# One fused attention and two-layer kernel: the sums of the first layer's weights, the order of the second block's output products, and when rows are loaded and summed

## The chip, the core and the metric

The kernel runs as one program on one core of a Trainium2 chip. The metric is device time in microseconds of one execution, from the inputs in the chip's main memory to the output there. The engines are named as in the profile: PE does matrix products and transposes (PEld is its load of the stationary operand, which overlaps), DVE, ACT and POOL do elementwise work, SP issues the transfers (DMA). Every engine works through its own instructions in the order in which the program lists them.

## What is computed

Eight batches of eight heads of 576 positions with 64 dimensions. Keys and values are pooled by eight, attention is taken over the 72 pooled positions, and the heads are laid side by side as 4608 rows of 512. Two feed-forward layers follow.

```python
k_p = k.reshape(B, H, Sp, 8, D).mean(axis=3);  v_p likewise
attn = softmax(scale * q @ k_p^T);  x = heads side by side of attn @ v_p      # 4608 x 512
gate = 1 / (1 + exp(-(x @ w_gate)));  val = x @ w_val                         # d_ff 1536
y = (gate * val) @ w_out
h = y @ w_in;  out = where(h > 0, h, exp(min(h, 0)) - 1) @ w_out2             # d_ff 2048
```

The six weight matrices arrive as 64-bit floats, which the kernel narrows itself on DVE (`convert`, and `prepared` for the second layer). A value that goes into a product is kept as two tiles, an upper part and the remainder (`split`: a copy on ACT, then a subtraction on POOL or DVE), and a product of two such values is three matmuls (`PASSES`).

## The kernel before

**Stages.** The rows are worked on in nine blocks of 512. Block 0's attention comes first, while weights arrive (to about 59 us). Then a loop over the twelve chunks `c` of the first layer's hidden columns handles block 0: gate product, value product, and, one chunk late, the output product (`emit_y`). In its first six rounds it also prepares block 1's attention. `plan()` lists what is placed before, between and behind the products of each round. From `LAG_FROM = 6` on, each round also runs two chunks of block 1's gate and value products ("side", L686 into `gw`): `side_gate` puts the sigmoid into a tile `sg1`, `side_val` multiplies and appends a store of the result to `g_dram`. `convert(1)` stands three times in a round and carries the narrowing of the weights three jobs further; it also counts down and issues the delayed stores in `stores`.

After the twelve rounds block 1 has only its output products left, the lagging products. A loop of twelve units does them (L711, into `acc`, weights reloaded as `wos`): `reload` brings one chunk of `g` from `g_dram`, `again` splits it, `emit_y` makes twelve matmuls. The attention of block 2 lies between them through lists `at2`: transposing queries (`emit_q`), scores (`emit_s`), `emit_exp`, `emit_norm`, transposing the probabilities (`emit_t`, with `keep_p` splitting them on ACT and DVE). All of these use one PSUM tile of two banks (`two_banks`, one buffer). The last two chunks of output products are kept as filler.

**Sums of weights.** Blocks 2 to 8 use a two-by-two scheme with seven products in place of eight. It needs sums and differences of weight blocks, which `form_weights` makes for each of twelve units `u`, in six steps each: two sums (L262), four differences half as wide (L264, L265, L269, L270), three splits, and stores to `t_dram`. It is a generator: `work(n)` runs its next n steps, and after it those of `prepared()`, which narrows and combines the second layer's weights. `formed[0]` says up to which pair of chunks the weights may be taken. Before, that is set after all twelve rounds, `work(4)` stands in each unit of the lagging loop, and what is left runs in block 2.

**Blocks 2 to 8.** After the attention products (`weighted`, L648 and L655) `form_x` forms the sums of the rows, through a chain of ACT and DVE operations that reads the products' PSUM banks. Then come twelve units `u` of seven steps `k`, each step being six matmuls into one of three banks (L1323) and a few output products as filler. The sum `u2` behind step 1 (L1338) must be done before step 3 opens the same bank. `thin_plan(m)` hangs the attention of the next block behind steps (u, k), through one PSUM bank (`one_bank`): `q_thin`, `s_thin`, `t_thin`, and for keys and values `load_kv`, `pool_k`/`pool_v` (a DVE reduction each), `place_v`, `k_first`, `k_last`. `WORK_AT` names the steps behind which `work()` stands, 35 in a block, and block 2 has 26 more. `load_t` fetches the stored sums two units ahead into two buffers of the tag "tt". Loaded rows of queries, keys and values, and the copies of the output products, share a tag "row" with three buffers; a load whose buffer is not free holds up SP and all that SP has behind it.

After block 8 the second layer runs (from about 1240 us), which the change does not touch.

## Time and profile before

| | |
|---|---|
| median of 3 runs (lowest to highest) | 2000.53 us (1994.74 to 2003.0) |
| profiled execution, own time | 1999.19 us |
| span of its instructions | 1996.3 us |
| busy: PE, DVE, ACT, POOL | 1821.4, 1096.5, 858.8, 634.0 us |
| mean granted PE clock (share of full speed) | 0.965 |
| attention of block 0 | 0 to 59.7 us |
| rounds 0 to 5, then 6 to 11 | 59.7 to 173.4, then to 291.3 us |
| lagging products, attention products of block 2 | 291.3 to 384 us |
| block 2, from the forming of its rows | 384 to 518.7 us |
| blocks 3 to 7, block 8 | 518.7 to 1120.1 us, to about 1240 us |
| second layer | to 1996.3 us |

The profile is of one execution. A busy PE need not be a PE at its peak: where the granted clock is below 1 each matmul takes longer. So a stretch is judged by three numbers of the windows view together: its length, the time that PE is busy in it, and the clock.

### The profile page before, as it was taken

To read this page: it belongs to the slowest core of one execution; us is meant where nothing else is said; L and a number is where in the kernel's file an instruction comes from. 1 tells how busy PE (TensorE), PEld (TensorE's weight loads), DVE (VectorE), ACT (ScalarE), POOL (GpSimd) and SP (SyncE) were. 2 spreads that over 40 slices of the span, in tenths; PEclk is the share of its full clock that TensorE was granted. 3 is DMA by queue.
4 is the path that set the end of the run, shared out by engine and by line. 5 is a ranking of instruction groups with operands and counts; after the bars stand their busy time and mean duration, and the time that the engine had idled before them with its cause. 6 is when DMAs were issued, how large, how long until landed. Compare 5 with 4: busy or idle time off the path is not lost. (4 is left out here: it accounts for less than half of the span.)

```text
span 1996.3 us, 28241 instructions
## 1 busy us (share of the span) xinstructions
PE 1821.4 (91%) x10308; PEld 1607.7 (81%) x10308; DVE 1096.5 (55%) x2055; ACT 858.8 (43%) x1776; POOL 634.0 (32%) x626
## 2 busy tenths in 40 slices
PE   5668986688899988989999989999999999999999
PEld 4556875577788877878888888999999999999998
DVE  6666625766767666767665655434544344443432
ACT  3343313334454443534445424445454444544543
POOL 2333315443434332433333422222222222222222
PEclk8878997799999999989999999999999999999999
DMA  7334426477676756656666696534334343343431
GB/s 200 102 115 146 153 88 217 150 225 233 231 230 222 226 191 220 220 193 224 204 229 201 211 347 217 209 111 175 111 137 182 114 174 111 133 165 135 161 111 50
DMA packets 154361, 353.10 MB, mean 177 GB/s; under 512 B 48112, under 2 KB 79856, under 8 KB 154224
## 3 DMA queue, kind: packets, MB, share of 16 engines
q1 hardware_dynamic: 154224, 351.32, 51.7%
q8 instruction: 81, 1.33, 0.3%
q14 instruction: 56, 0.46, 0.1%
HBM read 290.46 MB, written 60.82 MB: 176 GB/s over the span
## 5 line engine op out<-in xcount | busy, mean ns | idle before, releaser
L1444 PE MATMUL bank<-form,wr 128*128 128x384 f32 x2016 | 411.0, 338 | 1.1 <-DVE u L1477 0.7
L1444 PEld LDWEIGHTS bank<-form,wr 128*128 128x128 f32 x2016 | 366.5, 188 | 29.1 <-DVE u L1477 1.1
L711 PE MATMUL acc<-g,wos 128*128 128x512 f32 x1152 | 374.1, 410 | 15.1 <-ACT g L95 12.4
L1490 PE MATMUL oacc<-w2o,gc 128*128 128x512 f32 x1080 | 288.9, 393 | 0.4 <-POOL gc L96 0.4
L1490 PEld LDWEIGHTS oacc<-w2o,gc 128*128 128x128 f32 x1080 | 199.6, 187 | 30.4 <-POOL gc L96 0.8
L711 PEld LDWEIGHTS acc<-g,wos 128*128 128x128 f32 x1152 | 197.7, 197 | 29.6 <-ACT g L95 14.0
L1323 PE MATMUL pl<-s,wg 128*128 128x256 f32 x1008 | 159.8, 294 | 39.9 <-DVE u L1338 38.3
L96 POOL TENSOR_TENSOR gc<-ea,gc 128x384 fp32r<-128x384 f32 x96 | 98.0, 1021 | 299.0 <-ACT gc L95 295.9
L1323 PEld LDWEIGHTS pl<-s,wg 128*128 128x128 f32 x1008 | 138.5, 192 | 63.0 <-DVE u L1338 50.9
L96 POOL TENSOR_TENSOR g<-sg,g 128x512 fp32r<-128x512 f32 x108 | 145.9, 1362 | 134.7 <-ACT g L95 130.8
L96 POOL TENSOR_TENSOR gc<-pair,gc 128x384 fp32r<-128x384 f32 x96 | 97.8, 1019 | 260.3 <-ACT gc L95 239.8
L1323 PEld LDWEIGHTS pl<-a,wg 128*128 128x128 f32 x1008 | 142.8, 193 | 18.4 <-ACT r L1034 4.1
L1323 PE MATMUL pl<-a,wg 128*128 128x256 f32 x1008 | 153.4, 289 | 3.6 <-DVE xe L1028 2.1
L1323 PE MATMUL pl<-s,tt 128*128 128x256 f32 x1008 | 151.3, 286 | 1.7 <-DVE sg L1353 1.7
L1323 PEld LDWEIGHTS pl<-s,tt 128*128 128x128 f32 x1008 | 138.6, 189 | 11.3 <-DVE sg L1353 2.1
L1490 PE MATMUL oacc<-w2p,gc 128*128 128x512 f32 x540 | 143.1, 393 | 0.0
L95 ACT ACTIVATE g<-sg 128x512 fp32r<-128x512 f32 x108 | 67.7, 627 | 155.1 <-DVE sg L1363 114.4
L1490 PEld LDWEIGHTS oacc<-w2p,gc 128*128 128x128 f32 x540 | 99.8, 187 | 14.8
L1453 ACT ACTIVATE ea<-bank 128x384 f32<-128x384 f32 x48 | 23.6, 492 | 157.7 <-PE bank L1444 157.7
L1457 DVE SCALAR_TENSOR_TENSOR ea<-ea,bank 128x384 f32<-128x384 f32 x48 | 26.6, 554 | 117.2 <-ACT ea L1454 117.2
L1358 POOL TENSOR_TENSOR sg<-sg,u 128x256 f32<-128x256 f32 x42 | 37.0, 880 | 151.6 <-DVE u L1357 139.8
L686 PE MATMUL gv<-x,wg 128*128 128x512 f32 x288 | 78.6, 428 | 3.6 <-DVE x L96 3.6
(221 smaller groups left out, 3046.8 us busy)
## 6 DMA issues: line engine op xcount, KB each, us to landing
wr<-wd SPq DMA_DIRECT2D x96, 896.0 KB, 5.1
tt<-td SPq DMA_DIRECT2D x84, 768.0 KB, 5.2
wos<-wd SPq DMA_DIRECT2D x96, 512.0 KB, 5.2
rw<-in_moe_w_out_dram SPq DMA_DIRECT2D x22, 512.0 KB, 5.0
r<-yd SPq DMA_DIRECT2D x24, 384.0 KB, 9.0
out_dram<-po SPq DMA_DIRECT2D x36, 256.0 KB, 2.0
rw<-in_moe_w_in_dram SPq DMA_DIRECT2D x16, 512.0 KB, 5.0
wd<-rw SPq DMA_DIRECT2D x16, 512.0 KB, 5.1
```

The costliest lines, as they stand in the source:

```text
L95: nc.scalar.activation(out=dst_hi, in_=src, func=AF.Copy)
L96: eng.tensor_tensor(out=dst_lo, in0=src, in1=f32(dst_hi), op=ALU.subtract)
L686: nc.tensor.matmul(d, lhsT=w[:, i, a_w, j], rhs=x[j][:, a_x], start=(j == 0 and a_w == 0 and a_x == 0), stop=(j == KD - 1 and a_w == 1),)
L711: return lambda: nc.tensor.matmul(acc[m], lhsT=w[:, a_w, m * P:(m + 1) * P], rhs=g[:, a_g], start=(c == 0 and a_w == 0 and a_g == 0), stop ...
L1323: nc.tensor.matmul(src, lhsT=w(a_w, j), rhs=f_t[nm][:, j, a_x], start=opens and m == 0, stop=m == 5, skip_group_check=True,)
L1358: nc.gpsimd.tensor_tensor(out=c22, in0=c22, in1=u4, op=ALU.mult)
L1444: nc.tensor.matmul(bank[b ^ flip], lhsT=wp[q][a_w][:, w, j * P:(j + 1) * P], rhs=form_tile(s, a)[j][:, a_x], start=opens and n == 0, stop= ...
L1453: nc.scalar.activation(out=e, in_=src, func=AF.Relu, scale=-1.0)
L1457: nc.vector.scalar_tensor_tensor(out=e, in0=e, scalar=-1.0, in1=src, op0=ALU.add, op1=ALU.max)
L1490: return lambda: nc.tensor.matmul(acc[t + i], lhsT=g[c][:, a_g, i * P:(i + 1) * P], rhs=wo2[2 * q + e][a_w], start=opens and p == 0, stop= ...
```

## The change

It does five things.

1. `form_weights` starts inside rounds 7 to 11: `formed[0]` rises at the end of each round from 6 on, and rounds have `work(3)`, `work(4)` and, from 6 on, another `work(3)`. The lagging loop has `work(2)` in each of ten units, and a loop finishes the rest before `load_t`. Block 2 keeps only the 35 places. The sums and splits of one unit lie in one tile of the tag "tt" and are split in place; three stores take the place of two.
2. Of block 1's `g`, chunks 10 and 11 are not stored. They stay in the tiles `sg1`, which are now in the tags "p" and "qT" with one buffer each, and the lagging products start with them (`order`), with `wo[10]` and `wo[11]` still on the chip. The others are stored and reloaded two at a time. The delay of a store is two `convert`s in place of one.
3. Block 1's queries are loaded at the beginning into a tile `q1`.
4. The attention of block 2 moves to earlier units: scores at units 0, 2, 4, 6, normalisation at 1, 3, 5, 7, `emit_t` at 3, 5, 7, 9, and the key sums of batch 3 all come within the loop. `emit_k` for that batch takes the place of `k_first` at the start of block 2.
5. In `thin_plan` keys and values are loaded and summed one to a unit, `t_thin` is one step later with DVE's half as a step of its own (`t_low`), `q_thin` is one step later, and `WORK_AT` has other places, again 35.

```diff
-    g_dram = [dram.tile([P, NW], F32, ...) for i in range(C1)]
+    g_dram = [dram.tile([P, 2, NW], F32, ...) for i in range(C1 // 2 - 1)]
...
         for u in range(C1):
             cc, i = divmod(u, 2)
             while formed[0] <= cc:
                 yield
             wa, wb = wg[2 * cc], wg[2 * cc + 1]
-            ra, rb = plain_t().bitcast(F32), plain_t().bitcast(F32)
+            abc = wts.tile([P, 3, NW], F32, name="tw", tag="tt", bufs=2)
+            ra, rb, st = [abc[:, x] for x in range(3)]
...
-            kept()
             yield
             split(flat(wb[:, i, 0, 0:SQ]), flat(wb[:, i, 1, 0:SQ]), ra[:, lo])
...
             yield
-            two = raw_tile("t32")...
-            split(two[:, :, 0], two[:, :, 1], rb.rearrange("p (m f) -> p m f", m=2))
-            store(t_dram[u][:, 0:2], two)
-            yield
-            one = plain_t()...
-            split(one[:, 0], one[:, 1], ra[:, hi])
-            store(t_dram[u][:, 2], one)
+            kept()
+            split(st.bitcast(F32R), rb.bitcast(F32R), rb)
+            yield
+            split(ra[:, lo].bitcast(F32R), ra[:, hi].bitcast(F32R), ra[:, hi])
+
+            def keep_all(u=u, ra=ra, rb=rb, st=st):
+                for s, r in ((0, st), (1, rb)):
+                    nc.sync.dma_start(out=t_dram[u][:, 0:2, s], in_=r...)
+                nc.sync.dma_start(out=t_dram[u][:, 2]..., in_=ra)
+
+            keep.append(keep_all)
             yield
...
-            if i:
-                early[i - 1].append(lambda t=t: load_q(t))
...
+        q1 = spare("q1")
+        for i in range(TPW):
+            load_q(TPW + i, q1[:, i])
...
-            sg = wts.tile([P, NW], F32, name="sg1", tag="tt", bufs=2)
+            sg = at_p.tile([P, NW], F32, name="sg1", tag="qT" if c % 2 else "p")
...
-            stores.append([1, lambda: nc.sync.dma_start(out=g_dram[c], in_=sg)])
+            if c < C1 - 2:
+                stores.append([2, lambda: nc.sync.dma_start(out=g_dram[c // 2][:, c % 2], in_=sg)])
+            else:
+                back[c] = sg
...
             convert(1)
+            work(3)
             if late:
                 one = side_gate(second)
...
             if late:
                 side_val(*one)
             convert(1)
+            work(4)
             if pend is not None:
                 emit_y(0, *pend)
...
             if late:
                 side_val(*side_gate(second + 1))
+                work(3)
+                formed[0] = second // 2 + 1
...
+        again(C1 - 2)
+        while stores:
+            stores.pop(0)[1]()
+        reload(0)
         emit_k(SQ)
         emit_y(0, *pend)
-        while stores:
-            stores.pop(0)[1]()
+        reload(1)
         pt_now[0] = new_pt()
-        formed[0] = C1 // 2
         flush_y(0, acc)
         acc = outputs()
...
+        again(C1 - 1)
         t0 = SQ * TPW
+        emit_q(t0)
+        order = [C1 - 2, C1 - 1] + list(range(C1 - 2))
...
-            q_at, s_at, t_at = ((0, 1, 4), (1, 3, 6), (4, 5, 8), (6, 7, 10))[i]
-            put2(s_at, s2, t)
-            put2(s_at + 1, lambda t=t: emit_norm(t, p2[t]))
-            put2(t_at, emit_t, t)
-        for i in range(TPW):
-            put2((0, 1, 4, 6)[i], emit_q, t0 + i)
-            if i:
-                put2((0, 1, 4, 6)[i] - 1, load_q, t0 + i)
...
-        for c in range(C1):
-            again(c + 1)
-            reload(c + 2)
-            if c < C1 - 2:
-                emit_y(1, acc, g_of[c], c)
-            for f in at2[c]:
-                f()
-            work(4)
+            put2(2 * i, s2, t)
+            put2(2 * i + 1, lambda t=t: emit_norm(t, p2[t]))
+            if i + 1 < TPW:
+                put2(2 * i, load_q, t + 1)
+                put2(2 * i + 1, emit_q, t + 1)
+            put2(2 * i + 3, emit_t, t)
+        for c in range(NCH):
+            put2((1, 2, 3, 4, 5)[c], load_kv, "k", SQ + 1, c)
+            put2((4, 5, 6, 7, 8)[c], pool_k, SQ + 1, c)
+        put2(8, emit_k, SQ + 1)
+        put2(9, load_q, t0 + TPW)
+        for j, c in enumerate(order[:-2]):
+            if j % 2 == 1:
+                reload(j // 2 + 2)
+            for f in at2[j]:
+                f()
+            y = y_steps(acc, g_of[c], c, wo[C1 + c], first=j == 0, last=False)
+            for f in y:
+                f()
+            if j > 1:
+                next_wo()
+            again(order[j + 2])
+            work(2)
+        while stored[0] < C1:
+            work()
...
-                put(u + 2, 0, t_thin, t, 0, HP)
-                put(u + 2, 3, t_thin, t, HP, NCH)
-                put(u, 5, q_thin, t)
+                put(u + 2, 1, t_thin, t, 0, HP)
+                put(u + 2, 2, t_low, t, 0)
+                put(u + 2, 4, t_thin, t, HP, NCH)
+                put(u + 2, 5, t_low, t, HP)
+                put(u, 6, q_thin, t)
...
-                put(*((u - 1, 2) if i else (1, 4)), load_q, t)
-            if m < B:
-                for u, k, c in ((2, 0, 0), (4, 0, 1), (6, 0, 2), (8, 0, 3), (9, 0, 4)):
-                    put(u, k, load_kv, "v", m, c)
...
+                put(u, 0, load_q, t)
+            for c in range(NCH):
+                u = 2 * c + 2
+                if m + 1 < B:
+                    put(u - 1, 1, load_kv, "k", m + 1, c)
+                    put(u, 0, pool_k, m + 1, c)
+                if m < B:
+                    put(u, 2, load_kv, "v", m, c)
+                    put(u + 1, 1, pool_v, m, c)
+                    put(u + 1, 3, place_v, m, c)
             if m + 1 < B:
-                for u, k, c in ((9, 2, 0), (10, 1, 1), (10, 3, 2), (10, 5, 3), (11, 4, 4)):
-                    put(u, k, load_kv, "k", m + 1, c)
-                for u, k, c in ((10, 4, 0), (11, 0, 1), (11, 2, 2), (11, 3, 3)):
-                    put(u, k, pool_k, m + 1, c)
-                put(11, 5, k_first, m + 1)
+                put(10, 6, k_first, m + 1)
+                put(11, 2, k_last, m + 1)
...
-        WORK_AT = {(u, k) for u in range(2, C1, 2) for k in (1, 2, 4, 5)} | {(u, 3) for u in range(1, C1, 2)}
-        WORK_AT -= {(10, 2), (10, 4)}
-        WORK_AT |= {(0, 5), (1, 1), (1, 5), (1, 6), (4, 6), (6, 6), (8, 6), (9, 6), (10, 6), (11, 1), (11, 4)}
+        WORK_AT = {(u, k) for u in range(2, C1, 2) for k in (1, 3, 4, 5, 6)}
+        WORK_AT |= {(u, 3) for u in range(1, C1, 2)} | {(0, 5), (1, 1), (1, 5), (1, 6)}
...
-            else:
-                k_first(n + 1)
...
-                    if (u, k) in WORK_AT or n == SQ and k in (0, 2, 6):
+                    if (u, k) in WORK_AT:
                         work()
```

## Rows read from the trace of the kernel before

**Rows 1.** Windows: length, busy PE PEld DVE ACT POOL, PEclk, DMA share, GB/s
```profile
59.70:173.40 113.70, 75.58 (x359) 62.24 (x357) 81.98 (x116) 50.56 (x83) 43.94 (x34) 0.83 0.39 132
...
193.90:212.90 19.00, 19.00 (x85) 15.73 (x85) 11.74 (x17) 6.16 (x12) 6.43 (x6) 1.00 0.52 174
...
251.00:270.00 19.00, 19.00 (x86) 15.73 (x85) 7.30 (x11) 4.50 (x9) 6.04 (x6) 1.00 0.26 88
...
303.30:367.10 63.80, 46.15 (x188) 36.63 (x189) 38.17 (x56) 21.32 (x45) 33.78 (x30) 0.82 0.56 186
...
393.40:518.70 125.30, 109.44 (x722) 96.98 (x721) 87.10 (x175) 54.79 (x114) 47.99 (x51) 0.96 0.69 224
518.70:637.00 118.30, 110.05 (x770) 98.84 (x769) 82.15 (x171) 56.37 (x125) 45.48 (x49) 1.00 0.69 225
637.00:764.10 127.10, 113.75 (x778) 101.03 (x777) 83.09 (x169) 54.70 (x119) 44.55 (x47) 0.97 0.66 214
...
1004.00:1120.10 116.10, 110.44 (x765) 98.55 (x764) 69.87 (x158) 53.20 (x109) 37.35 (x33) 1.00 0.62 205
```

**Rows 2.** Timeline of PE: start, length, instruction xcount [idle before, its releaser]
```profile
118.63 1.09 PE L564 MATMUL atq<-ident,rq 128*128 128x128 f32 x4 [10.14 <-issue]
...
292.07 3.02 PE L711 MATMUL acc<-g,wo 128*128 128x512 f32 x12
303.29 5.42 PE L711 MATMUL acc<-g,wos 128*128 128x512 f32 x12 [8.20 <-ACT g L95]
...
334.73 0.63 PE L564 MATMUL atq<-ident,rq 128*128 128x128 f32 x4 [2.09 <-issue]
...
349.10 1.09 PE L564 MATMUL atq<-ident,rq 128*128 128x128 f32 x4 [5.12 <-issue]
...
354.08 1.14 PE L572 MATMUL ats<-kbd,qT 128*128 128x144 f32 x8
...
376.71 1.51 PE L648 MATMUL atv<-pt,vbd 128*128 128x128 f32 x6 [8.06 <-DVE pt L96]
...
384.05 2.34 PE L711 MATMUL acc<-g,wos 128*128 128x512 f32 x9
392.63 1.09 PE L1095 MATMUL atk<-ident,ks 128*128 128x128 f32 x4 [6.24 <-DVE xe L1028]
```

**Rows 3.** Timeline of DVE, same columns
```profile
117.77 0.76 DVE L585 TENSOR_TENSOR p<-ats,mx 128x576 f32<-128x576 f32 x1
...
298.22 0.69 DVE L738 COPY yo<-acc 128x512 f32<-128x512 f32 x1 [2.85 <-DMA yd<-yo]
298.83 1.28 DVE L262 TENSOR_TENSOR nt<-wg 128x512 f32<-128x512 f32 x2
...
317.81 2.89 DVE L262 TENSOR_TENSOR nt<-wg 128x512 f32<-128x512 f32 x2 [3.35 <-POOL t L96]
```

**Rows 4.** Groups by line, DVE: count, busy us, mean ns, idle before it by releaser
```profile
L262 DVE TENSOR_TENSOR nt<-wg 128x512 f32<-128x512 f32 x24 | 25.0, 1072 | 17.3 <-POOL t L96 10.7 <-POOL nt L96 6.4
```

**Rows 5.** Transfers by line: count, KB each, median us from issue to landing
```profile
td<-t SPq DMA_DIRECT2D x12, 512.0 KB, 6.5
```

**Rows 6.** Timeline of SP's queue, the start and block 4: time from first issue to last
```profile
24.09 5.94 SPq L419 DMA_DIRECT2D rq<-in_q_dram  x2
38.83 0.34 SPq L133 DMA_DIRECT2D rw<-in_moe_w_out_dram  x1
...
737.55 9.18 SPq L447 DMA_DIRECT2D rkv<-in_k_dram  x2
```

**Rows 7.** Timeline of ACT, the end of block 4
```profile
756.59 0.42 ACT L95 ACTIVATE rs<-nt 128x256 fp32r<-128x256 f32 x1 [5.24 <-DMA wd<-rw]
```

**Rows 8.** Waits of PE, rounds 0 to 5, then blocks: total us, times, longest
```profile
PE atq L564 <- issue: 21.2, 3, 10.1
...
PE pl L1323 <- DVE u L1338: 38.3, 38, 4.2
PE att L626 <- POOL p L619: 12.3, 24, 1.8
```

More of the change, by code (lines that the diff above doesn't have):

```diff
@@ L73, in fused_kernel @@
     y_dram = [dram.tile([P, KD, NB], F32, name=f"yd{i}", tag=f"yd{i}") for i in range(NBLK)]
-    g_dram = [dram.tile([P, NW], F32, name=f"gd{i}", tag=f"gd{i}") for i in range(C1)]
+    g_dram = [dram.tile([P, 2, NW], F32, name=f"gd{i}", tag=f"gd{i}") for i in range(C1 // 2 - 1)]
     t_dram = [dram.tile([P, 3, 2, HW], F32, name=f"td{i}", tag=f"td{i}") for i in range(C1)]
@@ L250, in kept @@
             keep.clear()
-        def store(dst, src):
-            keep.append(lambda: nc.sync.dma_start(out=dst, in_=f32(src)))
         for u in range(C1):
@@ L473, in pool_k @@
         n = size(c)
-        t = at_p.tile([P, 2, D], F32, name="ks", tag="kv", bufs=NCH)
+        t = at_p.tile([P, 2, D], F32, name="ks", tag="kv", bufs=NCH + 1)
         nc.vector.tensor_reduce(out=t[:n, 0], in_=r.rearrange("p (r d) -> p d r", r=POOL), op=ALU.add, axis=AX.X)
@@ L519, in sums_of @@
         if nm == "k":
-            t1 = at_p.tile([P, 2, D], F32, name="ks", tag="kv", bufs=NCH)
+            t1 = at_p.tile([P, 2, D], F32, name="ks", tag="kv", bufs=NCH + 1)
             for e in range(2):
@@ L526, in sums_of @@
             t4 = t4.bitcast(F32R)
-            t1 = at_p.tile([P, 2, D], F32R, name="vhl", tag="kv", bufs=NCH)
+            t1 = at_p.tile([P, 2, D], F32R, name="vhl", tag="kv", bufs=NCH + 1)
             split(t4[:, :, 0, :], t4[:, :, 1, :], four, nc.vector)
@@ L707, in emit_g, with y_steps @@
         return g
-    def y_steps(acc, g, c, w, by_tile=False):
+    def y_steps(acc, g, c, w, by_tile=False, first=None, last=None):
+        first = c == 0 if first is None else first
+        last = c == C1 - 1 if last is None else last
         def one(m, a_w, a_g):
@@ L712, in one @@
                 acc[m], lhsT=w[:, a_w, m * P:(m + 1) * P], rhs=g[:, a_g],
-                start=(c == 0 and a_w == 0 and a_g == 0), stop=(c == C1 - 1 and a_g == 1),
+                start=(first and a_w == 0 and a_g == 0), stop=(last and a_g == 1),
             )
@@ L874, in fused_kernel @@
         lag_ps = []
+        back = {}
         def side(c, i):
@@ L1074, in with_next @@
             return steps[:-1] + [f]
-        for c in (C1 - 2, C1 - 1):
-            fill += with_next(y_steps(acc, g_of[c], c, wo[C1 + c], c == C1 - 1))
+        for c in order[-2:]:
+            fill += with_next(y_steps(acc, g_of[c], c, wo[C1 + c], c == order[-1], False, c == order[-1]))
         filler(9)
@@ L1138, in t_thin, with t_low @@
                 turn_p(t, a, c)
-            keep_p(t, a, c0, c1)
+            o = t % TPW * P
+            hi, lo = [pt_now[0][:, h, c0:c1, o:o + P] for h in range(2)]
+            src = a[:, 0:(c1 - c0) * P].rearrange("p (c n) -> p c n", n=P)
+            nc.scalar.activation(out=hi, in_=src, func=AF.Copy)
+            halves_of[t, c0] = hi, lo, src
+        def t_low(t, c0):
+            hi, lo, src = halves_of.pop((t, c0))
+            nc.vector.tensor_tensor(out=lo, in0=src, in1=f32(hi), op=ALU.subtract)
         def thin_plan(m):
```

62 lines of the change are left out of this document (29 added, 33 removed).

## The prediction

> **What bounds the kernel now.** I read the windows by stage first [rows 1], because a mean over the whole span hides where PE is idle. From block 2 on PE is close to full: block 3 takes 118.30 us, of which PE is busy 110.05 at clock 1.00. So are the side rounds: in round 7 PE is busy all of its 19.00 us. Two stretches are not. In rounds 0 to 5 PE is busy 75.58 of 113.70 us at clock 0.83. The ten lagging units take most of a stretch of 63.80 us in which PE is busy 46.15 us at clock 0.82; DVE (38.17), ACT (21.32) and POOL (33.78) are not full either, so no engine bounds it. (The clock is the granted one as a share of 2.4 GHz; its levels are 1.2 and 2.4, so 0.82 is a mix of both, in stretches where PE pauses.) Next I read PE's timeline for what ended each pause [rows 2]. Where the releaser says only "issue", I looked in DVE's timeline [rows 3] for what ends just before, and the pauses turn out to be queues waiting for each other in program order.
>
> I sum against the profiled execution, 1999.19 us (2.9 us more than its span, 1.3 us less than the median).
>
> **A. Queries at the beginning: +1 us (0 to +3).** The pauses ahead of the query transposes in rounds 0 to 5 look like a late load, but are none. The longest is 10.14 us and ends at 118.63 [rows 2]. DVE ends its subtraction L585, the last reader of the two-bank scores tile, at 117.77 + 0.76 = 118.53 [rows 3]. The transposes write that tile; they wait for DVE, which has narrowing of weights ahead of the subtraction. An earlier load does not alter that, so I count no gain. The cost: two such loads hold SP for 5.94 us at the start [rows 6], and there are now five in place of these two, some 9 us more of SP. SP's next issue is a fetch at 38.83 us [rows 6], so most of it is covered; without that cover it would be the 9 us.
>
> **B. Sums inside rounds 7 to 11: +4 us (0 to +12).** By the steps, 10 of them in each of five rounds, 50 of 74 move here; a round gets 10/6 = 1.67 units. A unit on DVE is two sums and four differences of half the width. Two sums take 1.28 us with POOL idle, 2.89 us with POOL busy [rows 3], and 1.07 us each on average [rows 4]; I take half that for a difference. So a unit is 2.6, 4.3 or 5.8 us and a round gets 4.3, 7.2 or 9.7 us. Round 7 has DVE busy 11.74 of 19.00 us [rows 1], hence 16.0, 18.9 or 21.4 us of 19.0. Rounds 7 to 9 still narrow weights and are alike; round 10 has 7.30 us and stays at 17 us in the worst case. The mean fits exactly, the dear case costs 3 x 2.4 = 7 us, and a full DVE delivers the two multiplications that free PE's banks late now and then. I take 4; the top adds a few microseconds of a lower clock.
>
> Two sums at 1.28 us against 2.89 us [rows 3] are a question of ports. The Trainium skill, SBUF — State Buffer, section Who interferes with whom, says that a DVE instruction with two SBUF inputs and a GpSimd one that reads SBUF exclude each other for a whole instruction; both rows agree. By that rule alone, with a POOL subtraction in the way of every step, this part would be +7, not +4.
>
> Queues passed: SP gets 25 more issues here. A store of sums lands in 6.5 us [rows 5]; the unit that reuses the tile comes seven steps later, over half a round, so its first sum on DVE should find it free. If not, all of DVE's narrowing waits behind that sum. The sigmoids on ACT now wait for the store of the same tile from one round before, half as large and issued by the second `convert` after its multiplication, within about half a round of 19 us. Behind the sigmoid stand ACT's splits, for which the next output products wait. Both at zero, covered by the rest of the round; without that cover up to 6.5 us a round.
>
> **C. The lagging stretch: -17 us (-27 to -6).** Now the first lagging product starts at 303.29 after 8.20 us of idleness, behind a split of a reloaded chunk [rows 2]. Starting from the chip removes the reload, and next is late: the last copy of the finished block leaves PSUM at 298.22 + 0.69 = 298.91 [rows 3], then come a split and the query copy (which waits for it, as both use one tile), some 1.5 us, and scores of 1.14 us [rows 2]. That gives 301.5, 2 us earlier, and one tile's scores are done.
>
> Then ten units. In two of them PE has transposes of about 1.0 (four like them take 0.63 to 1.09), a pause until the two banks are evacuated, 2.09 at best, queries 0.6, scores 1.1 and two times twelve products [rows 2]. At full speed twelve take about 2.9 us (3.02 at 292.07), so the pair takes 10.5 us. Now twelve take 3.0 to 5.4, and the pause grows to 5.12 when DVE and ACT have sums ahead of the evacuation [rows 2]. With 20 steps of sums here, not 48, and L262's waits for POOL's tiles (10.7 + 6.4 us [rows 4]) gone by the new tiles, I take 12 us. Four pairs are 48, unit 0 is 4, unit 9 is 5: the products end at 358.5. The attention products are not held by the last probabilities any more (8.06 us idle [rows 2]), since these are transposed ahead of unit 9's products. They then take what they take now without that pause, 384.05 - 376.71 + 1.5 = 8.9 us, to 367.4 in place of 384.05: -17. At 10.5 us a pair it is -27; at today's pace of 6 us a unit, with only the last pause gone, -6.
>
> **D. The forming of block 2's rows: -4 us (-5 to -1).** `k_first` takes a PSUM bank that the forming chain reads to its end, and PE waits 6.24 us for it [rows 2]. Without it the first two steps of block 2 and their filler use banks freed early in the chain; step three still waits. Bounds: the whole pause or almost nothing.
>
> **E. Block 2 without sums: -8 us (-12 to -3).** It takes 125.30 us against 118.30 of block 3, with 15.9 us idle against 8.3, and clock 0.96 against 1.00, worth 0.04 x 109.44 = 4.4 [rows 1]. Idle and clock make 12. Not all is the sums, so I take 8.
>
> **F. Blocks 3 to 7: -10 us (-21 to +10).** In block 4, 127.10 us, two key loads without a free buffer stretch over 9.18 us in SP's queue [rows 6], the stores behind are late, and ACT waits 5.24 us for one [rows 7]. With one load to a unit a buffer is always free: -6 of the 8.8 us by which block 4 is longer than block 3. PE's waits for normalised probabilities, 12.3 us [rows 8], lose one step of over 1 us each: -9. Query transposes stand one step before the scores that need them, no longer two: +5 (24 times 0.2). The waits for L1338, 38.3 us [rows 8], lose the probability split ahead of them in DVE's queue and gain a reduction of some 1 us: 0. The low end is block 7, which sums no keys or values: 116.10 us [rows 1], 21 us in five blocks. The high end is the second rival.
>
> Sum: 1 + 4 - 17 - 4 - 8 - 10 = -34, hence 1965 us.
>
> **Rivals.** (1) *The lagging stretch keeps its pace.* The chain through two banks, not the sums, sets 6 us a unit: C at -6, 1976 us. For it: no engine is full there. Against it: the pause varies from 2.09 to 5.12 us, so something besides the chain lengthens it. (2) *The wait moves to L1338.* A reduction of about 1 us now stands right ahead of L1338 in five even units of five blocks; at 0.4 us each F becomes +10 with the losses above unrelieved, and E, which gets the same plan, -3: 1990 us. (3) *All of it falls well*: clock full in the lagging stretch, E and F near their ends: C -27, E -12, F -18, B +3: 1942 us. (4) *The early queries were the point*: if the "issue" pauses in rounds 0 to 5 (three, 21.2 us together [rows 8]) are loads after all, they vanish: 1944 us. The 0.1 us between DVE's end and PE's start speaks against it. (5) *Slower: DVE becomes the bound of rounds 7 to 11.* Place: POOL's added subtractions and DVE's sums exclude each other, the banks' multiplications come late, PE pauses and its clock falls, as in rounds 0 to 5 where DVE's queue paces PE. There 113.70 us hold 75.58 x 0.83 = 62.7 us of full-speed work [rows 1], a share of 0.55. Five rounds of 19.0 us at that share take 172, +77 for B: 2038 us. It decides against the change once B exceeds 38 us, that is, when a unit costs DVE some 9 us, not 4.3. The Trainium skill's rule on the shared port (SBUF — State Buffer, named under B) describes this mechanism; the trace bears it out in size only to 5.8 us a unit.
>
> **How the numbers follow.** Forecast 0.52 (its own range 1950 to 1980), rival 1 0.15, rival 2 0.12, rival 3 0.09, rival 4 0.04, rival 5 0.08. The range of 8 in 10 takes in rival 1, part of 2 and part of 3: 1943 to 1988. A measurement here can tell about 0.5%, 10 us. Faster by more: forecast, rivals 1, 3, 4 and half of 2: 0.85. Within: 0.07. Slower: 0.08.
>
> **What would show it.** Right: in rounds 7 to 11 PE stays busy with DVE near 18 of 19 us; the first lagging product about 301, the attention products of block 2 ending about 367 with no 8 us pause; block 2 near 118 us; no SP stretch like the 9.18 us one; rounds 0 to 5 unchanged, their "issue" pauses still ending with L585. Wrong: pauses of PE on `gw` in rounds 7 to 9 or DVE sums waiting for a store; lagging units still at 6 us; waits for L1338 well above 38 us in total; query transposes that wait for their load.

## The result and the profile after

The changed kernel takes **1947.1 us** (median of 4 runs, 1942.94 to 1951.63), the kernel before 1999.32 us beside it (1994.74 to 2003.0). The ratio is 0.974, 95% interval 0.971 to 0.9771: 52 us less. The profiled execution took 1951.63 us, its span is 1949.9 us, and it lies at the top of its runs, so that the stages below add up to 46.4 us, not 52.

| stage (us, from the profiled executions) | before | after | change | predicted |
|---|---|---|---|---|
| start, to the first gate product | 59.7 | 58.9 | -0.8 | A: +1 |
| rounds 0 to 5 | 113.7 | 116.0 | +2.3 | (in A) |
| rounds 6 to 11 | 117.1 | 119.0 | +1.9 | B: +4 |
| to the first lagging product | 12.8 | 9.5 | -3.3 | C: -17 |
| lagging products, to the first attention product | 63.8 | 55.1 | -8.7 | (in C) |
| attention products of block 2 | 17.0 | 5.0 | -12.0 | (in C) |
| to the third step's product of block 2 | 14.1 | 10.6 | -3.5 | D: -4 |
| rest of block 2 | 120.5 | 116.0 | -4.5 | E: -8 |
| blocks 3 to 7 | 601.4 | 581.8 | -19.6 | F: -10 |
| block 8 and second layer | 876.2 | 877.9 | +1.7 | 0 |

The windows of after (length, busy PE PEld DVE ACT POOL, PEclk, DMA share, GB/s) answer to [rows 1]: rounds 0 to 5, rounds of the sums, the lagging products, the attention products, then blocks 2 and 4.

```profile
58.90:175.00 116.10, 78.80 (x359) 64.72 (x357) 82.03 (x116) 50.55 (x83) 43.98 (x34) 0.81 0.38 125
195.40:214.40 19.00, 19.00 (x85) 15.73 (x85) 16.78 (x24) 7.33 (x15) 9.48 (x8) 1.00 0.51 158
...
252.40:271.90 19.50, 19.31 (x84) 15.65 (x84) 19.29 (x26) 7.01 (x16) 12.04 (x10) 1.00 0.40 135
303.50:358.60 55.10, 43.86 (x183) 34.96 (x183) 33.17 (x54) 18.70 (x44) 25.78 (x22) 0.85 0.66 222
358.60:363.50 4.90, 4.90 (x49) 4.26 (x47) 1.05 (x3) 1.88 (x4) 3.92 (x4) 1.00 0.16 54
374.20:490.20 116.00, 105.83 (x702) 94.98 (x701) 74.19 (x152) 47.07 (x102) 37.14 (x38) 0.94 0.67 213
...
607.40:726.20 118.80, 110.51 (x779) 98.20 (x778) 82.07 (x170) 55.61 (x122) 44.77 (x46) 1.00 0.69 227
```

Rounds 0 to 5 are as before: 116.0 us here, 113.8 to 114.6 in the runs below that leave them as they are. In the second row DVE has 16.78 us of work in a round of 19.00, in the third, round 10, 19.29 of 19.50: the sums fill it to the brim, and PE stays busy (19.00 and 19.31 us). The attention products now run at clock 1.00. Block 4 lost 8 us; block 2 still has its clock at 0.94.

The timeline of PE (start, length, instruction, count, [idle before, its releaser]), from the pause in rounds 0 to 5 to the forming of block 2's rows, answers to [rows 2]:

```profile
120.24 1.09 PE L566 MATMUL atq<-ident,q 128*128 128x128 f32 x4 [10.18 <-issue]
...
302.33 1.54 PE L574 MATMUL ats<-kbd,qT 128*128 128x144 f32 x8 [3.23 <-ACT qT L567]
303.50 4.41 PE L717 MATMUL acc<-g,wo 128*128 128x512 f32 x12
...
318.88 0.63 PE L566 MATMUL atq<-ident,rq 128*128 128x128 f32 x4 [2.09 <-issue]
...
331.07 1.09 PE L566 MATMUL atq<-ident,rq 128*128 128x128 f32 x4 [2.94 <-DVE pt L97]
...
358.61 0.78 PE L650 MATMUL xv<-pt,vbd 128*128 128x128 f32 x6
...
372.33 1.65 PE L1359 MATMUL pl<-a,wg 128*128 128x256 f32 x6 [4.12 <-ACT u L1369]
```

Waits of PE (total us, times, longest), answering to [rows 8], first in rounds 0 to 5, then in blocks 2 to 8:

```profile
PE atq L566 <- issue: 20.4, 3, 10.2
...
PE acc L717 <- ACT g L96: 19.1, 25, 2.2
PE pl L1359 <- DVE u L1374: 14.8, 15, 3.7
PE atq L1145 <- DMA rq<-in_q_dram: 3.4, 4, 1.0
```

The wait for the sum `u2` behind step 1 (L1338 before, L1374 now) fell from 38.3 to 14.8 us, and the wait for normalised probabilities (12.3 us) is gone. In their place stands one that the kernel before did not have in such number: 19.1 us in which output products wait for ACT's split of the gated product.

### The profile page after: what moved, and what is told of

It is laid out like the page before. It is cut to its first block, busy times and chain, and to the rows that moved or that the text cites. A ratio compares the mean times of both kernels' runs of the same rounds, so it can differ in the third digit from the quotient of the medians.

```text
span 1949.9 us, 28296 instructions
## 1 busy us (share of the span) xinstructions
PE 1812.7 (93%) x10308; PEld 1604.7 (82%) x10308; DVE 1097.3 (56%) x2053; ACT 858.4 (44%) x1775; POOL 638.4 (33%) x626
## 5 line engine op out<-in xcount | busy, mean ns | idle before, releaser
L717 PE MATMUL acc<-g,wos 128*128 128x512 f32 x1128 | 367.7, 409 | 22.5 <-ACT g L96 20.0
L717 PEld LDWEIGHTS acc<-g,wos 128*128 128x128 f32 x1128 | 191.0, 195 | 39.3 <-ACT g L96 26.1
L1359 PE MATMUL pl<-s,wg 128*128 128x256 f32 x1008 | 155.4, 290 | 15.2 <-DVE u L1374 14.8
L1359 PEld LDWEIGHTS pl<-s,wg 128*128 128x128 f32 x1008 | 142.6, 192 | 31.9 <-DVE u L1374 16.5
L97 POOL TENSOR_TENSOR g<-sg,g 128x512 fp32r<-128x512 f32 x98 | 129.8, 1341 | 102.2 <-ACT g L96 102.0
L96 ACT ACTIVATE g<-sg 128x512 fp32r<-128x512 f32 x98 | 61.6, 628 | 151.0 <-DVE sg L1399 117.8
L1526 PEld LDWEIGHTS oacc<-w2p,gc 128*128 128x128 f32 x540 | 99.8, 187 | 14.8
```

The lines of the kernel that those rows point to most:

```text
L96: nc.scalar.activation(out=dst_hi, in_=src, func=AF.Copy)
L97: eng.tensor_tensor(out=dst_lo, in0=src, in1=f32(dst_hi), op=ALU.subtract)
L717: return lambda: nc.tensor.matmul(acc[m], lhsT=w[:, a_w, m * P:(m + 1) * P], rhs=g[:, a_g], start=(first and a_w == 0 and a_g == 0), stop= ...
L1359: nc.tensor.matmul(src, lhsT=w(a_w, j), rhs=f_t[nm][:, j, a_x], start=opens and m == 0, stop=m == 5, skip_group_check=True,)
L1526: return lambda: nc.tensor.matmul(acc[t + i], lhsT=g[c][:, a_g, i * P:(i + 1) * P], rhs=wo2[2 * q + e][a_w], start=opens and p == 0, stop= ...
```

## The experiments

Times are medians; every ratio is against the kernel before, run beside it. That kernel's own median lay between 1996.75 and 2000.57 us from one experiment to the next, so a difference of two medians carries up to 4 us of that. Times of stages are from one profiled execution each.

**Sums back at their old place.** `form_weights` and its tiles as before the change, all 74 steps beside the lagging products and block 2; the probabilities of block 2 are back in their old tile too:

```diff
-            work(3)
...
-            work(4)
...
-                work(3)
...
-            work(2)
+            work(5 if j % 5 else 4)
...
-                    if (u, k) in WORK_AT:
+                    if (u, k) in WORK_AT or n == SQ and k in (0, 2, 6):
```

> The changed kernel with its sums of weights put back where they were: nothing in rounds 7 to 11, about 48 steps among the ten lagging units, the rest in block 2; everything else as changed. Theory 1, the sums in the queues of DVE, ACT and POOL are what lengthens the lagging stretch: from the first lagging product to the first attention product of block 2 it goes from 55 us to 64 to 70, rounds 6 to 11 get 2 us shorter, block 2 4 to 6 us longer, in all 1960 to 1970 us against 1947. Rival, the start from the chip and the new order of the attention free that stretch: it stays within 3 us of 55, in all 1947 to 1955 us.

Measured: 1998.92 us, ratio 1.0006 (0.9994 to 1.0018). The whole gain is gone: 52 us, more than either theory gave. By stage the rounds 6 to 11 give 2 us back, but the lagging products take 83.7 us and the attention products 10.6, 94.3 together; before the change they took 80.8, with the same sums beside them, and now 60.1. Block 2 takes 126.7. Blocks 3 to 7 keep their gain (582.6 us). The window of the lagging products, then the largest waits of PE and of DVE in it:

```profile
301.80:385.50 83.70, 45.05 (x183) 35.34 (x183) 45.48 (x74) 23.42 (x54) 33.91 (x33) 0.75 0.50 163
```
```profile
PE att L627 <- DVE p L586: 11.2, 3, 4.0
PE atk L489 <- ACT ks L477: 8.1, 2, 6.3
```
```profile
DVE nt L263 <- POOL t L97: 15.1, 4, 4.9
DVE nt L263 <- DMA td<-nt: 10.8, 2, 6.1
```

DVE is busy 45 of 84 us, so it is not full. It is late: the evacuation of two banks stands behind sums in its queue, and everything else of the stage passes through those banks. Much of the lateness is not the sums' own time: the first sum of a unit (L263) stands at the head of the queue for 25.9 us, until POOL's split or a store has freed its old tile. This run puts back place and tiles together, so it does not show what either is worth by itself. In sum the other edits are worth nothing without this one; by stage they gain 19 us in blocks 3 to 7 all the same, and lose 13.5 us from the first lagging product to the end of the attention products.

**Block 1's lagging products from chunk 0 again**, all twelve chunks stored and reloaded, in place of the two that remain on the chip:

```diff
-        order = [C1 - 2, C1 - 1] + list(range(C1 - 2))
+        order = list(range(C1))
```

> The changed kernel with the lagging products started from chunk 0 again: all twelve chunks of g stored and reloaded in pairs, all twelve of the output weights reloaded. Theory 1: the start is bound by the copies that empty the finished block's banks, so a reload ahead of it is worth 1 to 4 us, in all 1948 to 1952 us. Rival, the start from the chip is what frees the stretch: its first product comes 6 us or more later, in all 1955 us or more.

Measured: 1950.47 us, 0.9758 (0.9743 to 0.9772), which overlaps the interval of the change. In the trace the first lagging product comes 13.5 us behind the last gate product, not 9.5, and the last 4.93 us ahead of it PE waits for the reloaded output weights (`wos`), not for `g`. So 4 us at that place and 3 in the median, most of which this measurement can't tell from nothing.

**Old order of block 2's attention** (scores at units 1, 3, 5, 7, transposes three units later, the last behind the lagging products; query transposes and their loads at units that go with it):

```diff
-            put2(2 * i, s2, t)
-            put2(2 * i + 3, emit_t, t)
+            s_at, t_at = ((1, 4), (3, 6), (5, 8), (7, 10))[i]
...
```

> The changed kernel with the attention of block 2 at the units where it was (scores at 1, 3, 5, 7, normalising one later, transposed probabilities at 4, 6, 8 and behind the last unit). Theory 1: the pause ahead of the attention products of block 2 comes back with 5 to 8 us, the units themselves take as long as now, in all 1952 to 1957 us. Rival, order does not matter once the sums are gone: within 2 us of 1947.

Measured: 1958.82 us, 0.9803 (0.9788 to 0.9818). From the last gate product to the end of the attention products it takes 78.5 us in place of 69.6. The expected pause ahead of the attention products is 1.9 us only; the longest wait of PE in this stretch is that of a query transpose for its load:

```profile
PE atq L566 <- DMA rq<-in_q_dram: 6.1, 1, 6.1
```

Order and query loads together are worth some 9 to 12 us; how much is the order's alone this run does not show.

**Old `thin_plan` and unit steps in blocks 2 to 8**, and then its two halves one at a time: the places of the loads and sums of keys and values, and those of the transposes (`t_thin` with the low part directly behind it at steps 0 and 3, `q_thin` one step earlier, the query loads in the unit before). The old places of the unit steps (`WORK_AT`) are in the first run alone. Cut from the run of the transposes:

```diff
-                put(u + 2, 1, t_thin, t, 0, HP)
-                put(u + 2, 2, t_low, t, 0)
+                put(u + 2, 0, t_thin, t, 0, HP)
+                put(u + 2, 0, t_low, t, 0)
...
```

> The changed kernel with the plan of blocks 2 to 8 as before: keys summed in a bunch at the end of a block, probabilities transposed at step 0, query transposes at step 5, the old places of the work steps. Theory 1, the plan is what shortens blocks 3 to 7 from 601 to 582 us: they take 596 to 603 us again, SP's queue is held up by key loads, PE waits 25 to 40 us for L1374 (L1338 before) and some 12 us for normalised probabilities, in all 1960 to 1968 us. Rival, those blocks are shorter because they start with a better clock or in another phase of the second layer's narrowing: 582 to 588 us, in all 1947 to 1953 us.

> The changed kernel with the loads and sums of keys and values of the following blocks (thin_plan) at their places of before: ten loads in bunches, k_first at (11,5), the last key chunk in the next block. The other half of the plan (transposes of queries and probabilities, the split of the probabilities in two) and the places of the unit steps stay changed. The whole plan undone gave 1958: 18 us more in blocks 3 to 7 and 8.5 us less in block 2. Theory 1 (the bunched loads lose row buffers, as the 9.18 us in SP's queue show, in blocks 4 and 6, and the changed first key load takes a buffer from block 2's flush): blocks 4 and 6 get back their 126 and 121 us, block 2 its 108 to 110 us: 1950 to 1958. Theory 2 (the loads don't matter, the order of the probabilities and of DVE's queue does): blocks 3 to 7 as changed, 1944 to 1950.

> The changed kernel with the transposes of queries and probabilities in thin_plan at their places of before: t_thin at (u+2,0) and (u+2,3) with the low part straight behind the high part on DVE, q_thin one step earlier, load_q two units earlier. The loads and sums of keys and values stay changed. Theory 1 (the wait of PE for normalised probabilities, 12.3 us in the kernel before and gone after, comes back; and the wait for L1374, 14.8 us after against 38.3 before, grows back since the low part stands ahead of it in DVE's queue): blocks 3 to 7 get 9 to 25 us longer, block 2 stays: 1956 to 1972. Theory 2 (the loads' places make the gain, these are neutral): 1945 to 1952.

| | median us | ratio | block 2 | blocks 3 to 7 |
|---|---|---|---|---|
| after | 1947.1 | 0.974 | 116.0 | 581.8 |
| whole plan old | 1958.21 | 0.9802 (0.9786 to 0.9818) | 107.5 | 600.1 |
| loads and sums old | 1950.58 | 0.9773 (0.9751 to 0.9794) | 109.2 | 588.7 |
| transposes old | 1976.89 | 0.9901 (0.987 to 0.9932) | 119.3 | 602.4 |

The waits of PE in blocks 2 to 8, with the transposes at their old places, then with the loads and sums at theirs:

```profile
PE pl L1359 <- DVE u L1374: 44.0, 40, 2.8
PE att L628 <- POOL p L621: 16.3, 24, 1.8
```
```profile
PE acc L717 <- ACT g L96: 16.9, 24, 1.0
PE pl L1362 <- DVE u L1377: 13.4, 16, 3.2
```

With the old transposes both waits of the kernel before are back; with the old loads and sums they stay as in after. The transposes' places are worth 21 us in blocks 3 to 7, the loads' 7, each with the rest as changed. The two do not add up: with the whole plan old these blocks lose 18 us, not 28, and the wait for `u2` is 30.3 us, not 44.0. The old transposes thus cost more beside the new places of the loads and unit steps than beside the old ones; what the unit steps' places do by themselves no run shows. In block 2 the new loads cost 7 us: with the old ones it takes 109.2 us. The trace of after shows on ACT and PE where this begins:

```profile
389.43 0.60 ACT L749 ACTIVATE yo<-acc 128x512 f32<-128x512 f32 x1 [6.57 <-DMA yd<-yo]
```
```profile
390.60 0.74 PE L717 MATMUL acc<-g,wos 128*128 128x512 f32 x2 [2.21 <-ACT g L96]
```

The copies of the finished block and the loads of keys share three row buffers. The new plan loads a key chunk behind step (1, 1) of block 2, between two copies; the next copy waits 6.57 us for the store of an earlier one, and the split behind it on ACT makes PE wait 2.21 us. With the whole plan old, that copy does not wait. The pause is only a part of the 7 us, as block 2's window with the old loads and sums shows, beside that of after further up:

```profile
373.40:482.60 109.20, 101.83 (x701) 91.17 (x700) 73.21 (x147) 47.58 (x99) 37.46 (x38) 0.98 0.68 222
```

PE is idle 7.4 us in place of 10.2, and busy 101.8 us at clock 0.98 in place of 105.8 at 0.94: 3 us are idleness, 4 a lower clock.

**Queries in the rounds again** (one load a round, as before):

```diff
-            load_q(TPW + i, q1[:, i])
+            if i:
+                early[i - 1].append(lambda t=t: load_q(t))
```

> The changed kernel with block 1's queries loaded in the rounds again, one round ahead of their transposes, as before the change; nothing else. Theory 1 (part A: the loads were never what these pauses waited for): the pauses of 8.37 and 10.18 us ahead of the transposes keep their ends at DVE's subtraction L587, SP's 13.55 us at the start go, rounds 0 to 5 as now: 1944 to 1949. Theory 2 (rival 4: the loads in the rounds come late): the rounds get up to 20 us longer, or 1955 to 1970.

Measured: 1945.95 us, 0.9722 (0.9694 to 0.975): no difference. The two long pauses are 8.38 and 10.14 us, as with the early loads (8.37 and 10.18).

**Query transposes of block 1 one product later**, behind the round's value product in place of ahead of its gate product:

```diff
-            pre[i].append(lambda t=TPW + i: emit_q(t))
+            post[i].append(lambda t=TPW + i: emit_q(t))
```

> The changed kernel with one line moved: in rounds 0 to 3 a query tile is transposed behind the round's second gate product (list post), not ahead of its first (list pre). The loads stay at the beginning. In the changed kernel PE stands still ahead of these transposes for 4.42 us (released by the copy into kbd), 1.84, 8.37 and 10.18 us, the last two ending 0.1 us after DVE's subtraction L587. Theory 1 (the pauses are program order: the transposes need the two banks that DVE is late to read, and PE could do two gate products of some 3 us meanwhile): each pause shrinks by up to 6 us, the transposes of the probabilities (7.46 us behind L587 at 143.38) inherit some of it: 8 us less, 1935 to 1945. Theory 2 (DVE's queue, 82.0 of 116.1 us busy in rounds 0 to 5, sets these rounds whatever PE does): the pauses move to the transposes of probabilities or to the products, 1945 to 1952. Theory 3 (the loads set them): no pause changes its end, 1947 to 1952, with the transposes waiting for a DMA.

Measured: **1934.57 us**, 0.9685 (0.9655 to 0.9715), 12.5 us less than the change (11 by the ratios). The window of rounds 0 to 5 and the largest wait of PE in it:

```profile
57.80:162.00 104.20, 78.52 (x360) 63.03 (x360) 83.68 (x116) 50.20 (x84) 44.81 (x34) 0.89 0.42 139
```
```profile
PE att L628 <- DVE p L587: 6.1, 3, 2.7
```

PE and DVE do the same work, but the 20.4 us of waits put down to "issue" are spread over products that PE can make meanwhile, and the clock rises from 0.81 to 0.89. The pauses were neither loads nor a full DVE; they were the place of the transposes in PE's order.

**Sums four times over, in the rounds alone** (`dose[0]` is 4 until the last round is through, then 1):

```diff
+                for _ in range(dose[0]):
                     nc.vector.tensor_tensor(out=r, in0=f32(flat(w[:, i, 0])), in1=f32(flat(w[:, i, 1])), op=ALU.add)
```

> The changed kernel with each of the two sums of a unit (L262) computed four times over, only while the units are formed inside rounds 7 to 11 (some 8 units, six extra sums each, same values). It looks for the point from which DVE bounds these rounds. After: rounds 7 to 10 take 19.0 to 19.5 us with DVE busy 16.8 to 19.3, round 11 takes 22.9 with DVE busy 11.9. An extra sum is 1.07 us (POOL idle on average) to 1.45 us (half of 2.89 for two), so 6.4 to 8.7 us a unit and 10.7 to 14.5 us a round at 1.67 units. Theory 1 (DVE becomes the bound and PE pays only what DVE overflows by): four rounds at 27.5 to 33.8 us, round 11 at 22.6 to 26.4, so +36 to +60 us: 1983 to 2007. Theory 2 (rival 5 in its full price: PE pauses, the clock falls and the rounds go at the share of rounds 0 to 5, 0.55): +77 us, 2024. Theory 0 (the sums lie in gaps that nothing waits for, even fourfold): 1947 to 1952.

Measured: 1976.61 us, 0.99 (0.9878 to 0.9921): 29.5 us more than the change, below the range of either theory. Rounds 6 to 11 take 145.3 us, not 119.0. What a unit costs DVE is read from the groups by line in the rounds (count | busy us, mean ns | idle before), first of after, then of this kernel:

```profile
L261 DVE TENSOR_TENSOR tw<-wg 128x512 f32<-128x512 f32 x17 | 13.8, 829 | 1.4 <-DMA td<-tw 1.4
...
L268 DVE TENSOR_TENSOR tw<-tw 128x256 f32<-128x256 f32 x8 | 5.8, 726 | 0.3
L264 DVE TENSOR_TENSOR tw<-tw 128x256 f32<-128x256 f32 x8 | 5.3, 668 | 0.3
...
L267 DVE TENSOR_TENSOR tw<-tw 128x256 f32<-128x256 f32 x8 | 3.6, 445 | 0.2
...
L263 DVE TENSOR_TENSOR tw<-tw 128x256 f32<-128x256 f32 x8 | 3.4, 424 | 0.2
```
```profile
L263 DVE TENSOR_TENSOR tw<-wg 128x512 f32<-128x512 f32 x64 | 55.5, 872 | 1.6
```
```profile
235.00:255.00 20.00, 13.70 (x50) 10.80 (x51) 19.33 (x27) 5.65 (x12) 9.12 (x8) 0.74 0.61 209
255.00:275.00 20.00, 14.94 (x58) 11.48 (x57) 19.69 (x29) 5.64 (x12) 9.06 (x8) 0.91 0.27 88
```

A unit costs 2 x 0.83 + 0.73 + 0.67 + 0.45 + 0.42 = 3.9 us of DVE in the change, and with eight sums 8 x 0.87 + 2.0 = 9.0 here. DVE has become the bound (19.33 and 19.69 of 20 us, last two rows), and PE waits for its multiplications (19.3 us in three waits). Eight units at 5.1 us more are 41 us of DVE by this reckoning. By the windows of rounds 7 to 11 DVE is busy 37 us more; 26.3 of them show as time, and 11 went into time in which DVE had stood idle, 15.5 us in after, most of it in round 11.

**A better version, in three steps.** First the kernel with the later query transposes, and in block 2 alone the old places of loads and sums:

```diff
+            if m == SQ + 1:
+                for u, k, c in ((2, 0, 0), (4, 0, 1), (6, 0, 2), (8, 0, 3), (9, 0, 4)):
+                    put(u, k, load_kv, "v", m, c)
...
```

> The changed kernel with the query transposes behind the second gate product (the kernel that gave 1934.6) and, in block 2 alone, the loads and sums of keys and values at their places of before; blocks 3 to 7 keep the new places. With the old places everywhere block 2 took 109.2 us, with the new ones 116.0 (114.9 in the kernel that this builds on), and blocks 3 to 7 were 7 us longer. Theory 1 (in block 2 the first key load takes a row buffer that the copies of the finished block need, and that is the whole difference): block 2 at 108 to 110 us, the rest as it was: 1927 to 1931. Theory 2 (block 2's loss comes from elsewhere, or is handed on to block 3): 1932 to 1937.

Measured: 1931.48 us, 0.9663 (0.9637 to 0.9688); block 2 takes 110.1 us in place of 114.9, block 3 takes 119.1 in place of 117.3. The medians differ by 3 us, within the intervals, and part of block 2's gain is handed on to block 3. The waits of PE in its blocks 2 to 8:

```profile
PE acc L717 <- ACT g L96: 16.9, 24, 0.9
PE pl L1374 <- DVE u L1389: 12.7, 16, 2.6
```

Then the work step of odd units moved from step 3 to step 5, against the waits for ACT's split:

```diff
-        WORK_AT |= {(u, 3) for u in range(1, C1, 2)} | {(0, 5), (1, 1), (1, 5), (1, 6)}
+        WORK_AT |= {(u, 5) for u in range(3, C1, 2)} | {(1, 3)} | {(0, 5), (1, 1), (1, 5), (1, 6)}
```

> The kernel of z1 with one more edit: in odd units the step that prepares the second layer's weights stands behind step 5 in place of step 3. In the changed kernel PE waits 19.1 us in 25 waits for the second part of the gated product on ACT (acc<-g), most of them 0.5 to 0.95 us in even units. Theory 1 (the work step's split on ACT, ahead of the table load and of the row sums' increment, delays ACT and DVE there): the waits fall below 10 us, blocks 2 to 7 are 6 to 12 us shorter, 1918 to 1925. Theory 2 (ACT is late for another reason, the split simply stands behind the copy of u2): 1926 to 1933.

Measured: 1935.96 us, 0.9683 (0.9662 to 0.9704), no gain. The waits of PE in blocks 2 to 8:

```profile
PE pl L1374 <- DVE u L1389: 19.9, 29, 3.2
PE acc L717 <- ACT g L96: 14.3, 24, 0.9
```

The wait for ACT's split fell by 2.6 us and that for DVE's sum rose by 7.2: it only changed places. DVE's timeline of the first step's kernel at one of these waits, and POOL beside it, shows who is late:

```profile
391.25 0.75 DVE L606 TENSOR_REDUCE sm<-p 128x8 f32<-128x576 f32 x1
392.47 0.20 DVE L615 RECIPROCAL sm<-sm 128x8 f32<-128x8 f32 x1 [0.47 <-ACT sm L614]
...
393.36 1.21 DVE L1414 TENSOR_TENSOR sg<-sg,u 128x256 f32<-128x256 f32 x1
...
394.94 0.43 DVE L1419 TENSOR_TENSOR sg<-sg,u 128x256 f32<-128x256 f32 x1
```
```profile
393.14 1.15 POOL L621 TENSOR_TENSOR p<-p,sm 128x576 f32<-128x576 f32 x1 [1.34 <-PE pl L1374]
```

DVE sums a row, ACT adds 1e-9, and DVE waits for it with L1413 and L1414 queued behind, whose result ACT must split for PE. Last step: the first step's kernel without that addition.

```diff
-        nc.scalar.activation(out=sm, in_=sm, func=AF.Copy, bias=1e-9)
```

> The kernel of z1 (query transposes behind the second gate product; in block 2 alone the loads and sums of keys and values at their old places) without L614, the instruction on ACT that adds 1e-9 to the row sums between DVE's sum (L606) and its reciprocal (L615). A row sum holds an exp(0) = 1, so that in float32 the increment changes no bit of it. In the blocks of z1 DVE stands idle ahead of the reciprocal 24 times, 0.27 to 1.57 us, 15.6 us together; behind the reciprocal in DVE's queue stand the multiplications whose results ACT splits for the output products, and PE waits for these splits 24 times, 0.44 to 0.94 us, 16.9 us together (acc<-g, released by ACT g). In one such place DVE waits 0.47 us and PE 0.61. Theory 1 (DVE's wait for ACT is handed on to PE): the 16.9 us fall to between 3 and 8, the blocks get 8 to 13 us shorter: 1918 to 1924. Theory 2 (PE's waits come from ACT's own order, or the next wait in DVE's queue takes over, as in z2 where the waits for the first sum of the pair, L1389 there, grew from 12.7 to 19.9 us): 1928 to 1934.

Measured: **1918.06 us**, 0.9605 (0.958 to 0.963), 13.4 us less than the first step (11.6 by the ratios) and 29 less than the change. The waits of PE in its blocks:

```profile
PE pl L1373 <- DVE u L1388: 12.2, 16, 2.7
PE acc L716 <- ACT g L96: 10.2, 24, 1.0
```

The wait fell by 6.7 us, to 10.2 and not below 8, and the other did not grow. Blocks 2 to 7 are 10.6 us shorter in the profiled executions, and the span 12.6; the start and rounds 0 to 5, where DVE has the same detour, are 3 us shorter, though the start alone varies by as much from run to run. Without the addition ACT has an instruction less as well, so the run alone doesn't separate its own time (0.19 us on ACT) from DVE's wait for it. For the wait speaks that ACT, too, stands idle less for the multiplication behind it in DVE's queue: 113.6 us in place of 120.0, in 41 waits each.

## Why the prediction was right, and where its steps failed

The direction and most of the mechanisms held; the sum, -34, came out short of the measured -52 (-46 in the profiled executions). 1947.1 us lies 4 us inside the range that takes in the rivals (1943 to 1988), and outside the forecast's own, 1950 to 1980. The terms were further off than the sum shows: C, F and B together were 19 us too pessimistic, E 3.5 us too hopeful. By its steps:

**A held.** +1 forecast, +1.5 by the stages, less than the 2.3 us by which runs with the same start and rounds differ, and none by the run with the loads back in the rounds. The five loads hold SP's queue for 13.55 us at the start and the next fetch goes out at 39.10, as late as before (38.83). DVE's L587 ends at 119.38 + 0.76 = 120.14, and the transposes start at 120.24, as in [rows 2, 3]:

```profile
24.97 13.55 SPq L421 DMA_DIRECT2D q<-in_q_dram  x5
39.10 0.34 SPq L134 DMA_DIRECT2D rw<-in_moe_w_out_dram  x1
```
```profile
119.38 0.76 DVE L587 TENSOR_TENSOR p<-ats,mx 128x576 f32<-128x576 f32 x1
```

Rival 4 (the early queries were the point) fell with that, though its 1944 us is nearer to the result than the forecast. But the step stopped too soon: it took the pause as given by DVE's queue, and the run with the transposes behind the value product shows that PE's own order gave it 12.5 us of room.

**B held, a little better than forecast.** +1.9 us for +4. A unit costs DVE 3.9 us (4.3 taken), and the rounds take what is free in DVE; the dear case of 5.8 us, with +7 for this part, did not come. The stores were hidden as said: DVE waits 1.4 us in the rounds for a tile of sums that is still being stored. Rival 5 gave 2038 us and a turn to a loss when a unit costs 9 us. At 9.0 us, in the run with fourfold sums, the rounds lose 26.3 us and the kernel is still 1% faster than before. The mechanism is as told in that DVE is full and PE's clock falls to 0.74, but it was over-priced: it spread the low share of rounds 0 to 5 over all five rounds, while round 11 has 11 us of DVE free and the clock recovers between pauses (0.91 in the next window).

**C was right in its mechanism and too small: -24 for -17.** Put back by the 3.5 us by which after enters the stage later, the first lagging product starts at 300.0 (301.5 forecast), the products take 55.1 us (57), the attention products 5.0 (8.9). So 1.5, 1.9 and 3.9 us. The last term is the mis-sized one: I kept the present duration of the attention products without its pause, but that duration was at clock 0.52, as a window of before shows that I had not read; in after the same products run at 1.00, with no pause ahead of them:

```profile
367.10:384.10 17.00, 8.94 (x51) 7.85 (x49) 12.71 (x19) 5.53 (x14) 9.28 (x9) 0.52 0.66 225
```

Both bounds were reckoned wrongly: four pairs at 10.5 us in place of 12 make -23, not -27, and the last pause alone is 8.06 us, not 6. Rival 1 (the stretch keeps its pace, with the sums blameless) fell: with the sums and their tiles back the stretch takes 94.3 us. I also took the parts as adding up; they do not. Sums and tiles back cost all 52 us by themselves, the attention's old order with its loads 12.

**D held**: -3.5 for -4. The first step of block 2 and a filler start early (365.87), and the second step waits 4.12 us for ACT's copy. I had let the third step be the first to wait.

**E was half right: -4.5 for -8.** Without its sums block 2 can take 110 us, as the first step of the better version shows, which would have been -10. The 4.4 us of clock that the forecast counted did not come: the clock there is 0.94 after, 0.96 before. The forecast named the new plan for blocks 3 to 7 alone and did not cost its loads in block 2, where they meet the copies of the finished block. That is the +6 that is missing; the trace shows 3 us of it as idleness and the rest as clock.

**F fell as a sum of terms: -19.6 for -10.** The loads are worth -7 (run with the old ones), -6 forecast, though with the whole plan old it is block 4 that is long. The waits for normalised probabilities went altogether, -12.3 for -9. The query waits cost 3.4 us for +5. The failed step is "the waits for L1338 ... 0". I set the loss of the probability split ahead of it against a reduction of 1 us, and called it even. With the split back the waits are 44.0 us in 40, without it 14.8 in 15: -29, with all else as changed. The reduction costs next to nothing once the split is away: with the loads and sums at their old places the waits are 13.4 in 16. Part of what that freed went into a wait that I had not listed as a candidate, ACT's split of the gated product: 19.1 us, against 2.6 with the transposes at their old places. Rival 2 (the wait moves to L1338, 1990 us) was wrong about where. Rival 3 (all falls well, 1942) is, with rival 4, nearest in time; its C and F came nearest to what was measured, its E did not.

## What to carry to other kernels

Work that hides in a free engine's time must also be free of what that engine's queue holds up behind it: the same sums cost 2 us where DVE's queue carried narrowing, and with their old tiles 52 where it carried the evacuation of the only two banks. There a sum that waited for its tile at the head of the queue held up the banks as well as one that worked (25.9 us of such waits). When a pause goes, reckon the work behind it at the clock that it will then have. And where a wait comes from program order, move the waiting instruction behind a product that could have been made meanwhile, and take out of a chain between two engines any step that changes no bit.

## What the runs showed of the hardware

**Twelve products behind a pause of 2 to 3 us took 1.0 to 1.6 us longer, at a lower granted clock.** The windows of four groups of twelve lagging products in after: the first after 3.23 us of idleness and scores of 1.5 us, the second behind 2.09 us and four transposes, the third straight behind the second, the fourth behind 2.94 us and four transposes:

```profile
303.50:307.90 4.40, 4.40 (x14) 3.24 (x13) 3.79 (x7) 0.77 (x2) 0.00 (x0) 0.65 0.97 294
...
319.26:323.70 4.44, 4.44 (x16) 3.53 (x15) 3.11 (x7) 0.73 (x2) 1.26 (x1) 0.62 0.49 177
324.57:327.40 2.83, 2.83 (x15) 2.30 (x14) 2.43 (x3) 1.00 (x3) 1.99 (x2) 1.00 0.00 0
331.81:335.60 3.79, 3.79 (x15) 3.08 (x14) 1.47 (x3) 0.91 (x3) 1.15 (x1) 0.73 0.59 183
```

The same dozen takes 3.8 to 4.4 us at a mean clock of 0.62 to 0.73 (a mix of 1.2 and 2.4 GHz) and 2.8 us at 1.00. The longer pause is not the dearer one.

**DVE's multiplication L1414 took 1.21 us, the equal L1419 0.43** (rows above). POOL was normalising from 393.14 to 394.29, and L1414 ended 0.28 us behind that, at 394.57. The Trainium skill, SBUF — State Buffer, section Who interferes with whom, says that a DVE instruction with two inputs in SBUF blocks until a GpSimd one that reads SBUF is through, if that was issued first. The trace agrees in kind; that 0.28 us is less than the whole 0.43 says little, as POOL's times are rough in these profiles.
